# Splitting MoE weight chunks into two halves on ScalarE and VectorE alone, without GpSimd

## The chip, the cores and the metric

The kernel runs on one core of one Trainium2 chip. The metric is the device time of one execution in microseconds. Before the change the median of three runs is 1549.79 us (1549.74 to 1550.39).

## What is computed

The reference chains three layers on 1792 tokens (4 sequences of 448) with a model width of 768:

```python
scores = einsum('bhij,hg->bgij', scale * q @ k.T, w_pre)   # attention, heads mixed
attn   = softmax(scores); attn = einsum('bhij,hg->bgij', attn, w_post); x = attn @ v
expert_idx = argmax(x @ w_gate, axis=1)                    # MoE, top 1 of 8 experts
out[mask]  = gate_w * (maximum(x[mask] @ w1[e], 0) @ w2[e])
g = h * sigmoid(h); y = g @ w_out      # h = out @ w_in     # dense FFN, width 2048
```

All inputs are float32. To keep accuracy on TensorE, every operand of a large product is split in two: a high half rounded to the fp32r type, and a low half, which is the operand minus its high half. A product is then three matmuls (`mm3`, lines 797 to 799: high by high, high by low, low by high).

## The kernel before, in words

The program has three stages: attention (its instruction order comes from a list scheduler, class `Plan`), the MoE layer and the dense FFN (both in `experts`, in the order in which the code is written).

In the MoE stage tokens are sorted by expert and worked on in tiles of 128, called slots; 18 slots are run. A slot needs four weight chunks of its expert: c = 0 and 1 are the two halves of `w1[e]` (products `mm1`, 18 matmuls of 512 columns each), c = 2 and 3 the two halves of `w2[e]` (`mm2`, 24 matmuls of 384 columns). A pair (slot, c) is an item. `slots` writes the items out in a fixed order: for a slot s of the middle it is (s, 0), (s-1, 2), (s, 1), (s-1, 3).

Each chunk has one raw buffer (`wraw`, 128 x 3072 floats) into which SP loads it (`wload`, line 842); where the next slot has the same expert, the load is skipped by a condition. A load is issued as soon as the chunk's predecessor in that buffer has been split. `wsplit` (lines 849 to 856) splits a raw chunk in two steps of 1536 columns (`HW`), each into a pair of tiles, `rhi` and `rlo`, from a ring of four pairs. `ahead` runs the splits two items (LOOK = 4 steps) ahead of the matmuls.

In one step the columns are divided at `PC` = 1152: ACT rounds the first 1152 (line 852) and DVE subtracts them (line 854); POOL rounds the other 384 (line 853) and subtracts them (line 855).

The same engines also do this around the items, in the order of the code:

- PE transposes the gathered tokens (`xT`, 6 transposes, line 872) and the hidden layer (`hT`, 4 each); ACT rounds the result to `xhi` or `hhi` and DVE subtracts to `xlo` or `hlo` (`split`, lines 860 and 861).
- ACT applies relu to a finished `mm1` (h, line 891) and the gate to a finished `mm2` (y, line 909). Each of these waits for the end of its item, and the casts for the item after the next stand behind it in ACT's queue.
- POOL issues the gather of tokens two slots ahead (line 865) and the scatter of a finished y (line 911). There is one buffer for y.
- `hook` places routing tables into the stream: `gate_prep` and `gate_table` near slot 0, `order_prep` (lines 703 to 721 and 786) behind item (1, 3). Later it places the first loads and transposes of the FFN; the loads of y for it are issued from ACT's queue.

Of the kernel before, what the change touches and what calls it, by code (L numbers as in the profile page):

```python
# [9 lines left out]
F32 = mybir.dt.float32  # L10
# [4 lines left out]
ALU = mybir.AluOpType  # L15
# [16 lines left out]

P = dict(GHN=3, TDN=1, CVN=2, RAW=4, DB=2, G=4, GH=3, GL=2, WM=3, E=4, CC=384, GLN=2, WMN=1, slack=0.05, rx=3.2,
         relay=7.0, ghi=3.5, glo=2, mix1=4.6, mx=2.5, exp=3.2, rz=1.9, wm=0.8, ev=3, qk=0.25, qkx=1.85, av=0.5,
         avs=0.7, rows=0.9, tr=-5.8, trh=1.625, trs=0.9, ld=6.1, lv=0.5, c0=-4.0, c1=3.0, cp=0.3, cl=8, PC=1152)


P_WARM = 16
# [42 lines left out]
def fused_kernel(ctx: ExitStack, tc: tile.TileContext, q, k, v, w_pre, w_post, wg, w1, w2, w_in, w_out, cst, out):  # L81
# [30 lines left out]
    with tc.tile_pool(name="pre", bufs=1) as pre:  # L112
# [21 lines left out]
        nc.vector.tensor_tensor(out=wp1l, in0=wp1, in1=wp1h.bitcast(F32), op=ALU.subtract)  # L134
    attention(tc, nc, q, k, v, x_d, oh, cum, zsum, c_e8, ident, (wp1h, wp1l), wp2, wg_sb, ((w_in, wi_d), (w_out, wo_d)))
    experts(tc, nc, x_d, y_d, w1, w2, wi_d, wo_d, out, ident, oh, cum, zsum,
            (tri, c_rid, c_tid, c_val, c_s, c_m), idx_g, idx_s, idx_o, gate_s, es_i)


class Plan:  # L140
    """Orders operations by list scheduling: each engine takes the most urgent operation that can start."""

    LAT = 0.2

# [657 lines left out]
def experts(tc, nc, x_d, y_d, w1, w2, wi_d, wo_d, out, ident, oh, cum, zsum, consts,  # L802
# [7 lines left out]
    with outer:  # L810
# [33 lines left out]
        def pair():  # L844
            return ring.tile([128, HW], F32R, name="rhi", tag="rhi"), ring.tile([128, HW], F32R, name="rlo", tag="rlo")

        PC = P["PC"]

        def wsplit(s, c, half):
            hi, lo = pair()  # L850
            src = raw[c][:, half * HW:(half + 1) * HW]
            nc.scalar.copy(hi[:, :PC], src[:, :PC])  # L852
            nc.gpsimd.tensor_scalar(out=hi[:, PC:], in0=src[:, PC:], scalar1=1.0, scalar2=1.0, op0=ALU.mult, op1=ALU.mult)  # L853
            nc.vector.tensor_tensor(out=lo[:, :PC], in0=src[:, :PC], in1=hi.bitcast(F32)[:, :PC], op=ALU.subtract)  # L854
            nc.gpsimd.tensor_tensor(out=lo[:, PC:], in0=src[:, PC:], in1=hi.bitcast(F32)[:, PC:], op=ALU.subtract)  # L855
            tiles["w", s, c, half] = (hi, lo)

        def split(dst, src):
# [135 lines left out]
        def slots(s0, s1, hook):  # L994
# [7 lines left out]
            def ahead(n):  # L1002
                while nsplit[0] < min(n, 2 * len(plan)):
                    a, c = plan[nsplit[0] // 2]
                    hf = nsplit[0] % 2
                    wsplit(a, c, hf)
                    if hf == 1 and a + 1 < s1:
                        wload(a + 1, c)
                    nsplit[0] += 1
# [123 lines left out]
```

## Time and profile before

| what | value |
|---|---|
| median of three runs | 1549.79 us |
| span of the profiled execution | 1548.0 us |
| attention | from 0 to about 630 us |
| MoE stage, from the first `mm1` to the first FFN matmul | 635 to 1057 us |
| FFN | 1057 to the end |
| mean DMA rate over the span | 121 GB/s |

The page gives the profiled execution by its span; the runs were timed by themselves, and their median is 1.8 us above it. PE is TensorE's matmul, PEld its weight load, which runs beside the matmul before it. A matmul's record is longer than its distance to the next one, because matmuls are pipelined, so gaps are read from the weight loads. Idle time is put down to the event that came last before the engine went on.

### The profile page before, as it was taken

How to read it: one execution, taken by the hardware profiler on the slowest of the kernel's cores; microseconds unless marked ns; L12 is line 12 of the kernel's file. 1: busy time of each engine (PE TensorE's matmuls, PEld its weight loads, DVE VectorE, ACT ScalarE, POOL GpSimd, SP SyncE). 2: the span in 40 equal slices, each digit the busy share in tenths (PEclk: the TensorE clock that was granted, in tenths of full speed). 3: DMA queues.
4: the chain of work that ended last, by engine and by line, in shares of the span. 5: the costliest groups of instructions: out<-in, count | busy, mean ns of one | idle time of the engine just before them, and what ended most of it. 6: DMA issues, size and time to landing. Idle time of an engine off the chain costs nothing. (4 is left out here: it accounts for less than half of the span.)

```text
span 1548.0 us, 25390 instructions
## 1 busy us (share of the span) xinstructions
PE 1441.1 (93%) x9030; PEld 1231.5 (80%) x9030; DVE 1079.0 (70%) x1774; ACT 850.7 (55%) x1600; POOL 811.9 (52%) x877
## 2 busy tenths in 40 slices
PE   7999999999999998897988888988999999999997
PEld 4677667767776777786767667878999999999997
DVE  5798889889998996876766656774445445454464
ACT  4566766677776665354555645653444444444453
POOL 6577577647665774889999998991000000000000
PEclk9999999999999999898999999999999999999999
DMA  7455565656564556205934266407101000010000
GB/s 158 157 159 168 123 213 162 165 147 201 165 149 155 175 164 218 94 21 181 325 104 142 94 229 231 145 11 261 65 11 52 11 31 21 11 42 11 1 31 21
DMA packets 137074, 186.77 MB, mean 121 GB/s; under 512 B 51100, under 2 KB 108736, under 8 KB 136944
## 3 DMA queue, kind: packets, MB, share of 16 engines
q1 hardware_dynamic: 129536, 155.74, 32.8%
q0 software_dynamic: 5392, 23.86, 4.4%
q10 hardware_dynamic: 2016, 5.51, 1.1%
q8 instruction: 73, 1.20, 0.3%
q14 instruction: 57, 0.47, 0.1%
HBM read 186.64 MB, written 30.67 MB: 140 GB/s over the span
## 5 line engine op out<-in xcount | busy, mean ns | idle before, releaser
L854 DVE TENSOR_TENSOR rlo<-wraw,rhi 128x1152 fp32r<-128x1152 f32 x144 | 233.6, 1662 | 127.5 <-ACT rhi L852 127.4
L986 POOL DMA_INDIRECT out_dram<-ob,idx_o x14 | 13.5, 963 | 473.0 <-DVE ob L984 458.5
L855 POOL TENSOR_TENSOR rlo<-wraw,rhi 128x384 fp32r<-128x384 f32 x144 | 204.6, 1421 | 12.0
L423 PE MATMUL m<-WM,E 120*112 120x120 f32 (+1 forms) x1440 | 186.9, 275 | 14.3 <-DVE a_sb L254 6.5
L423 PEld LDWEIGHTS m<-WM,E 120*112 120x112 f32 (+1 forms) x1440 | 162.7, 178 | 41.7 <-issue 18.1
L361 POOL TENSOR_TENSOR GL<-G,GH 120x448 fp32r<-120x448 f32 (+1 forms) x139 | 169.5, 1225 | 11.8 <-ACT GH L254 3.2
L852 ACT CAST rhi<-wraw 128x1152 fp32r<-128x1152 f32 x144 | 158.4, 1151 | 9.6 <-DMA wraw<-in_moe_w_dram 9.6
L797 PE MATMUL b<-fxhi,rhi 128*128 128x384 f32 (+1 forms) x480 | 157.7, 328 | 4.2 <-ACT rhi L860 4.2
L799 PE MATMUL b<-fxhi,rlo 128*128 128x384 f32 (+1 forms) x480 | 157.7, 329 | 0.5 <-DVE rlo L861 0.5
L798 PE MATMUL b<-fxlo,rhi 128*128 128x384 f32 (+1 forms) x480 | 156.8, 327 | 0.0
L956 DVE TENSOR_TENSOR sg<-b,sg 128x384 f32<-128x384 f32 (+1 forms) x80 | 42.4, 530 | 155.6 <-ACT sg L954 155.6
L797 PE MATMUL b<-rhi,gh 128*128 128x384 f32 x436 | 148.4, 340 | 0.0
L954 ACT ACTIVATE sg<-b 128x384 f32<-128x384 f32 (+1 forms) x80 | 37.7, 471 | 199.4 <-PE b L799 199.3
L799 PE MATMUL b<-rhi,gl 128*128 128x384 f32 x436 | 146.8, 337 | 0.0
L798 PE MATMUL b<-rlo,gh 128*128 128x384 f32 x436 | 146.6, 336 | 0.0
L389 ACT ACTIVATE E<-m,mx 120x448 f32<-120x448 f32 x180 | 113.5, 632 | 48.8 <-DVE mx L379 29.6
L410 POOL TENSOR_SCALAR WM<-wp,rz 120x120 f32<-120x120 f32 x180 | 86.3, 487 | 93.0 <-DVE rz L400 40.1
L853 POOL TENSOR_SCALAR rhi<-wraw 128x384 fp32r<-128x384 f32 x144 | 129.1, 897 | 2.6 <-PE b L799 1.7
L798 PE MATMUL b<-rlo,hhi 128*128 128x384 f32 x288 | 101.0, 351 | 20.4 <-POOL rlo L855 20.1
L379 DVE TENSOR_REDUCE mx<-m 120x1 f32<-120x448 f32 x180 | 108.6, 614 | 10.9 <-PE m L799 10.1
L798 PE MATMUL b<-rlo,xhi 128*128 128x512 f32 x216 | 91.1, 422 | 15.8 <-POOL rlo L855 13.4
L797 PE MATMUL b<-rhi,hhi 128*128 128x384 f32 x288 | 100.7, 350 | 1.7 <-POOL rhi L853 1.7
(194 smaller groups left out, 3689.5 us busy)
## 6 DMA issues: line engine op xcount, KB each, us to landing
wraw<-in_moe_w_dram SPq DMA_DIRECT2D x76, 1536.0 KB
G<-S SPq DMA_DIRECT2D x176, 210.0 KB
D<-in_moe_w_in_dram SPq DMA_DIRECT2D x32, 384.0 KB
D<-in_moe_w_out_dram SPq DMA_DIRECT2D x32, 384.0 KB
wi_d<-CM SPq DMA_DIRECT2D x32, 192.0 KB
wo_d<-CM SPq DMA_DIRECT2D x32, 192.0 KB
win<-wi_d SPq DMA_DIRECT2D x8, 768.0 KB
wout<-wo_d SPq DMA_DIRECT2D x8, 768.0 KB
```

The source lines that it names most:

```text
L361: G.tensor_tensor(out=t[:n], in0=x[:n], in1=hi[:n].bitcast(F32), op=ALU.subtract)
L379: V.tensor_reduce(out=mx[:n], in_=tiles["m1", i, g][:n, :S], axis=AX.X, op=ALU.max, negate=True)
L389: A.activation(out=t[:n], in_=tiles.pop(("m1", i, g))[:n, :S], func=ACTF.Exp, bias=tiles.pop(("mx", i, g))[:n], accum_out=tiles["z", i, g ...
L410: G.tensor_scalar(out=wm[:n], in0=wp2[:n], scalar1=rz, scalar2=1.0, op0=ALU.mult, op1=ALU.mult)
L423: nc.tensor.matmul(p[:, c, :, :nr], x[:n, c * CH:(c + 1) * CH], wm[:n, :, :nr], start=True, stop=True)
L797: nc.tensor.matmul(p, lh, rh, start=first, stop=False)
L798: nc.tensor.matmul(p, lh, rl, start=False, stop=False)
L799: nc.tensor.matmul(p, ll, rh, start=False, stop=last)
L852: nc.scalar.copy(hi[:, :PC], src[:, :PC])
L853: nc.gpsimd.tensor_scalar(out=hi[:, PC:], in0=src[:, PC:], scalar1=1.0, scalar2=1.0, op0=ALU.mult, op1=ALU.mult)
L854: nc.vector.tensor_tensor(out=lo[:, :PC], in0=src[:, :PC], in1=hi.bitcast(F32)[:, :PC], op=ALU.subtract)
L855: nc.gpsimd.tensor_tensor(out=lo[:, PC:], in0=src[:, PC:], in1=hi.bitcast(F32)[:, PC:], op=ALU.subtract)
```

## The change

`wsplit` no longer divides the columns. ACT rounds all 1536 columns of a step and DVE subtracts all 1536; POOL's two instructions are gone, and with them the constant `PC`. Everything behind `wsplit` stands four lines earlier in the changed kernel (the subtract is line 851, `split` 856 and 857, the gather 861, the scatter 907).

```diff
-        PC = P["PC"]
-
         def wsplit(s, c, half):
             hi, lo = pair()
             src = raw[c][:, half * HW:(half + 1) * HW]
-            nc.scalar.copy(hi[:, :PC], src[:, :PC])
-            nc.gpsimd.tensor_scalar(out=hi[:, PC:], in0=src[:, PC:], scalar1=1.0, scalar2=1.0, op0=ALU.mult, op1=ALU.mult)
-            nc.vector.tensor_tensor(out=lo[:, :PC], in0=src[:, :PC], in1=hi.bitcast(F32)[:, :PC], op=ALU.subtract)
-            nc.gpsimd.tensor_tensor(out=lo[:, PC:], in0=src[:, PC:], in1=hi.bitcast(F32)[:, PC:], op=ALU.subtract)
+            nc.scalar.copy(hi, src)
+            nc.vector.tensor_tensor(out=lo, in0=src, in1=hi.bitcast(F32), op=ALU.subtract)
             tiles["w", s, c, half] = (hi, lo)
```

POOL, one slot of the MoE stage before the change: a gather, the roundings and subtracts of four chunks, and a scatter in their midst.

```order
L865 DMA xg<-x_d,idx_g 128x768
L853 TENSOR_SCALAR rhi<-wraw_7940 128x384
L855 TENSOR_TENSOR rlo<-wraw_7940,rhi 128x384
L853 TENSOR_SCALAR rhi<-wraw_7940 128x384
...
L855 TENSOR_TENSOR rlo<-wraw_7939,rhi 128x384
L911 DMA y_d<-y,idx_s 1792x768
L853 TENSOR_SCALAR rhi<-wraw_7941 128x384
L855 TENSOR_TENSOR rlo<-wraw_7941,rhi 128x384
```

The same place on POOL in the changed kernel, two slots of it:

```order
L710 TENSOR_SCALAR A_8667<-cs,lo_8662 120x128 x5
L861 DMA xg<-x_d,idx_g 128x768
L907 DMA y_d<-y,idx_s 1792x768
L861 DMA xg<-x_d,idx_g 128x768
L907 DMA y_d<-y,idx_s 1792x768
```

Sixteen instructions of a slot have left POOL's queue; a gather is now directly followed by a scatter.

DVE, the subtracts around item (1, 3) in the changed kernel, up to the first instructions of `order_prep`:

```order
L851 TENSOR_TENSOR rlo<-wraw_7940,rhi 128x1536 x2
L851 TENSOR_TENSOR rlo<-wraw_7942,rhi 128x1536 x2
L857 TENSOR_TENSOR hlo<-b_8545,hhi 128x512
L851 TENSOR_TENSOR rlo<-wraw_7939,rhi 128x1536 x2
L857 TENSOR_TENSOR xlo<-b_8602,xhi 128x384
L857 TENSOR_TENSOR xlo<-b_8608,xhi 128x384
L851 TENSOR_TENSOR rlo<-wraw_7941,rhi 128x1536 x2
L857 TENSOR_TENSOR hlo<-b_8652,hhi 128x512
L703 CAST pi_8659<-pos 120x16
```

Before the change the same rows stand in the same order, with 128x1152 in the subtracts of weights. No instruction of PE, ACT or DVE has changed its place; xlo stands behind both subtracts of a chunk, as before.

## Rows read from the trace of the kernel before

**Rows 1.** The page, busy time by engine over the whole span

```profile
PE 1441.1 (93%) x9030; PEld 1231.5 (80%) x9030; DVE 1079.0 (70%) x1774; ACT 850.7 (55%) x1600; POOL 811.9 (52%) x877
```

**Rows 2.** Windows: length, busy PE, PEld, DVE, ACT, POOL; clock; DMA share; GB/s

```profile
635.00:1057.00 422.00, 364.71 (x1810) 308.01 (x1808) 284.55 (x245) 226.93 (x296) 387.77 (x326) 0.96 0.41 140
858.90:882.50 23.60, 19.90 (x101) 16.27 (x100) 15.70 (x13) 12.54 (x17) 22.56 (x19) 1.00 0.23 79
1066.00:1540.00 474.00, 471.71 (x2819) 470.03 (x2817) 242.82 (x350) 203.79 (x350) 12.52 (x13) 1.00 0.11 38
```

**Rows 3.** Waits of PEld, 635 to 1058 us: total us, times, longest

```profile
PEld b L798 <- POOL rlo L855: 50.8, 46, 2.0
PEld b L797 <- POOL rhi L853: 9.9, 7, 6.3
PEld b L872 <- ACT h L891: 5.4, 2, 3.1
...
PEld b L799 <- DVE xlo L861: 3.3, 9, 0.5
```

**Rows 4.** Timeline, 678 to 694 us: start, length, engine, instruction, idle before it

```profile
678.34 3.20 DVE L854 TENSOR_TENSOR rlo<-wraw,rhi 128x1152 fp32r<-128x1152 f32 x2 [1.13 <-ACT rhi L852]
...
686.70 0.19 PEld L798 LDWEIGHTS b<-rlo,xhi 128*128 128x128 f32 x1 [1.70 <-POOL rlo L855]
...
687.82 0.19 PEld L797 LDWEIGHTS b<-rhi,hhi 128*128 128x128 f32 x1
...
687.97 2.20 ACT L852 CAST rhi<-wraw 128x1152 fp32r<-128x1152 f32 x2
...
689.15 3.43 DVE L854 TENSOR_TENSOR rlo<-wraw,rhi 128x1152 fp32r<-128x1152 f32 x2 [2.76 <-ACT rhi L852]
...
692.42 0.19 PEld L797 LDWEIGHTS b<-rhi,xhi 128*128 128x128 f32 x1
...
693.10 0.19 PEld L799 LDWEIGHTS b<-rhi,xlo 128*128 128x128 f32 x1 [0.37 <-DVE xlo L861]
```

**Rows 5.** Groups of instructions, 635 to 1058 us: busy us, mean ns, idle before

```profile
L854 DVE TENSOR_TENSOR rlo<-wraw,rhi 128x1152 fp32r<-128x1152 f32 x142 | 231.0, 1667 | 126.0 <-ACT rhi L852 125.9
L852 ACT CAST rhi<-wraw 128x1152 fp32r<-128x1152 f32 x142 | 156.2, 1151 | 0.0
...
L861 DVE TENSOR_TENSOR hlo<-b,hhi 128x512 fp32r<-128x512 f32 x36 | 24.4, 677 | 0.0
...
L891 ACT ACTIVATE h<-b 128x512 f32<-128x512 f32 x36 | 21.6, 599 | 101.4 <-PE b L799 85.1 <-DMA y_d<-y,idx_s 16.3
...
L860 ACT CAST hhi<-b 128x512 fp32r<-128x512 f32 x36 | 21.1, 587 | 0.0
...
L861 DVE TENSOR_TENSOR xlo<-b,xhi 128x384 fp32r<-128x384 f32 x36 | 18.2, 543 | 1.1 <-ACT xhi L860 1.1
...
L860 ACT CAST xhi<-b 128x384 fp32r<-128x384 f32 x36 | 15.5, 486 | 2.2 <-PE b L872 2.2
```

**Rows 6.** Groups of instructions in the FFN, 1066 to 1540 us

```profile
L861 DVE TENSOR_TENSOR rlo<-win,rhi 128x768 fp32r<-128x768 f32 x78 | 74.7, 958 | 15.7 <-ACT rhi L860 13.7
...
L860 ACT CAST rhi<-win 128x768 fp32r<-128x768 f32 x78 | 64.9, 833 | 0.0
```

**Rows 7.** Line 854, nanoseconds min/median/max; then line 911, scatter of y

```profile
L854 DVE TENSOR_TENSOR rlo<-wraw,rhi x144: 1343/1652/2179, 631.7 to 1044.8; 128x1152 fp32r<-128x1152 f32 x144
...
DMA to landing us min/median/max: 3.1/4.1/8.1
```

**Rows 8.** Timeline of DVE, `order_prep`: first and last of eight instructions

```profile
697.92 0.40 DVE L703 CAST pi<-pos 120x16 int32<-120x16 f32 x1
...
703.03 0.53 DVE L721 TENSOR_TENSOR B<-sel,tidv 120x224 fp32r<-120x224 f32 x1
```

**Rows 9.** Windows, columns as in rows 2: a stretch in which experts change

```profile
745.00:765.00 20.00, 19.76 (x107) 17.05 (x106) 14.32 (x12) 11.35 (x15) 19.04 (x17) 1.00 0.98 339
```

**Rows 10.** Waits of ACT, 635 to 1058 us

```profile
ACT h L891 <- DMA y_d<-y,idx_s: 16.3, 2, 9.4
```

More of the change, by code (lines that the diff above doesn't have):

```diff
@@ L34 @@
          relay=7.0, ghi=3.5, glo=2, mix1=4.6, mx=2.5, exp=3.2, rz=1.9, wm=0.8, ev=3, qk=0.25, qkx=1.85, av=0.5,
-         avs=0.7, rows=0.9, tr=-5.8, trh=1.625, trs=0.9, ld=6.1, lv=0.5, c0=-4.0, c1=3.0, cp=0.3, cl=8, PC=1152)
+         avs=0.7, rows=0.9, tr=-5.8, trh=1.625, trs=0.9, ld=6.1, lv=0.5, c0=-4.0, c1=3.0, cp=0.3, cl=8)
 P_WARM = 16
```

## The prediction

> **What bounds the kernel now.** I read the page's busy line first: over the whole span TensorE is busy 93%, VectorE (DVE) 70%, ScalarE (ACT) 55%, GpSimd (POOL) 52% [rows 1]. That average hides three stages, so the next view is the table of windows [rows 2]. In the MoE stage, 635 to 1057 us, POOL is busy 388 of 422 us (92%), DVE 285 (67%), ACT 227 (54%). One slot of that stage (an expert tile of 128 tokens, 858.9 to 882.5) takes 23.6 us, and POOL is busy 22.56 us of it. The dense FFN behind it (1066 to 1540) is TensorE without a gap at a granted clock of 1.00; the change does not touch it.
>
> Then the waits of TensorE's weight loads in the MoE stage [rows 3]. All rows of that answer come to 84.7 us; four stand here. 50.8 us, in 46 waits, end with POOL's low-half subtract and 9.9 us with POOL's rounding: 60.7 us for POOL. So without waits the stage would be 422 - 84.7 = 337 us, 18.7 us per slot. One stretch shows that POOL is late alone and not merely last [rows 4]: TensorE starts again at 686.70, after 1.70 us on POOL's subtract. At that time chunk (slot 2, c 1) is being multiplied; DVE took its two low halves from 678.34 to 681.54, five microseconds earlier.
>
> **The change, part by part.** *Removed:* 144 roundings and 144 subtracts of 384 columns on POOL. Only gathers, scatters and five table instructions stay there in this stage, so the waits on POOL go: **-60.7 us**.
>
> *Widened on ACT:* a cast of 1152 columns takes 1151 ns [rows 5], one of 768 takes 833 ns in the FFN [rows 6]: 0.83 ns a column, so 1536 take about 1.47 us, 0.32 more. Per slot 8 x 1.47 + 2 x 0.599 (h) + 2 x 0.587 (hhi) + 2 x 0.486 (xhi) + about 1.2 for the two y (taken as long as h) = 16.3 us, under 18.7.
>
> *Widened on DVE:* the subtract of 1152 takes 1343 ns at least, 1652 in the middle, 2179 at most [rows 7]. In the FFN, where POOL is nearly idle, 768 columns take 958 ns [rows 6]. The line through 958 and 1343 gives 1.74 us for 1536. The upper bound is the stage's mean rate, 1667 ns for 1152 [rows 5], so 2.22 us. I take 1.74, because the low values are those without POOL at work. Per slot: 8 x 1.74 + 2 x 0.677 + 2 x 0.543 [rows 5] = 16.4 us.
>
> Both stay under TensorE's 18.7, but only if the order of the chain holds. I replay one handover [rows 4]. Item (slot 1, c 3) starts at 687.82, my zero. ACT's casts for the item after it, (3, 0), begin at 0.15, and DVE at 1.33, just behind the first cast. With 1536 columns the first cast ends at 1.62, low half A at 3.39, B at 5.14. Item (3, 0) starts at 4.60 (692.42) and wants A at once and B some 2 us later: both are in time. Where fewer transposes lie between two items the margin is smaller by up to 0.8 us, still about 0.4 us. So both engines hide under TensorE; without the cover each slot would cost at most what DVE has over 18.7, which is the first rival.
>
> *What is late next:* xlo. On DVE it stands behind halves A and B. At 693.10 TensorE's third weight load waited 0.37 us for it, and started 5.28 after my zero. Now it comes at 5.14 + 0.54 + 0.06 = 5.74, 0.46 later. Sixteen slots have this place: **+7 us** (0 to +10; zero if TensorE has fallen behind by then anyway).
>
> *The index tables:* eight small DVE instructions from 697.92 to 703.56 [rows 8] stand ahead of slot 2's and 3's subtracts. POOL's table work and splits hid them (one wait on POOL's rounding alone is 6.3 us [rows 3]). They hold DVE 5.6 us; about 1 us of that goes with POOL's splits, and margin and DVE's own idle time cover some 1.5. **+3 us** (0 to +5).
>
> *Weight loads:* a chunk's load is issued when its predecessor is split and has then some 13 us of a slot. An expert's four chunks are 4 x 1536 KB = 6.3 MB, gather and scatter 0.8 MB. In 745 to 765, where experts change in three slots running, DMA moves 339 GB/s at 0.98 busy [rows 9]: 7.1 MB take 20.9 us against a slot of 18.9. Three such slots give 6 us, half of it absorbed by the early issue: **+3 us** (0 to +7).
>
> *Scatter of y:* POOL now issues it at once. It lands 3.1 to 8.1 us after issue [rows 7], and ACT's next write to y comes two items, some 9 us, later, so it just fits. Where ACT itself waits to issue a load of y (16.3 us in two waits [rows 10]), the present loss at TensorE, 5.4 us on h [rows 3], stays. Less POOL traffic beside the gate tables at the start is worth about **-1 us**. The other waits I leave as they are.
>
> Sum: -60.7 + 7 + 3 + 3 - 1 = -48.7. The profiled execution spans 1548.0 us; the median of the runs is 1549.8, so 1.8 us more. 1548.0 - 48.7 + 1.8 = **1501 us**.
>
> One rule speaks against the change. By the rows, POOL has the smallest share of the whole span and the change loads two busier engines. The Trainium skill (Perfetto Trace Analysis, Identifying the Most-Contended Engine) says to relieve the engine with the highest occupancy first; read over the span, it would see nothing to win here, and the time would stay at 1549.8. The same page says that the most contended engine may change between regimes, and [rows 2] show that it does.
>
> **The rivals.** *First, DVE stays slow and becomes the bound.* If the 2179 ns are not POOL's doing but DMA's or the wide tile's, a subtract takes 2.22 us and a slot 8 x 2.22 + 2.44 = 20.2 us, 1.5 more for some 15 slots: 1523 us. For it: the median of 1652 is far over 1343. Against: the 958 ns beside an idle POOL. The Trainium skill (SBUF — State Buffer, Who interferes with whom) says that a DVE instruction with two SBUF inputs and a GpSimd instruction that reads SBUF block each other, the second until the first ends. By that rule the spread is POOL's, and it goes; the trace agrees as far as 1343 to 2179 shows.
>
> *Second, the loads bind at every change of expert.* There are seven such slots; 20.9 against 18.9 plus a late first chunk each, 2 to 3 us: 14 to 18 us more, 1516 us. For: 0.98 busy in [rows 9]. Against: single changes have half the traffic per microsecond.
>
> *Third, slower.* Place: ACT's queue, where the next casts stand behind h or y, which wait for the end of an item. If a split cannot be ready two items ahead, as the four-pair ring intends, each item shows TensorE the chain of cast 1.47 + subtract 1.74 + 0.7 of activation and handover = 3.9 us. Over 72 items that is 281 us in place of 84.7: about 1746 us. It decides where the mean wait of an item passes 84.7 / 72 = 1.18 us. Against it: the replay.
>
> *Fourth, it does not do what it says:* POOL's waits are put down to the last comer, and DVE would be late just behind it: 1549 us. Against: the five microseconds at 681.54.
>
> **How the numbers follow.** Main case 0.72, 1488 (xlo, tables and loads cost nothing) to 1510 (their upper ends): 1501 is its sum. DVE-bound 0.10 at 1523; loads 0.12 at 1516; slower 0.03; nothing 0.03. A change of 0.2% is about what measurement can tell here. The main case and the first two rivals are faster: 0.94; within 0.2%: 0.03; slower: 0.03. The range 1484 to 1524 takes in the first two rivals, and below the main case 4 us of what the half-clock stretches in the stage (0.96 granted on the mean [rows 2]) may give back.
>
> **What would show it.** Right: no waits on POOL in the MoE stage, POOL under 20% busy there; casts at 1.47 and subtracts at 1.74 us; ordinary slots near 19 us; waits on xlo the largest repeated row; a stage of some 373 us; an FFN as long as before. Wrong: subtracts over 2 us, waits on DVE's low half in every slot, ACT waiting for weights, or slots over 20 us where no expert changes.

## The result and the profile after

The changed kernel takes 1488.24 us (median; 1487.63 to 1490.55) against 1550.09 us for the kernel before in the same runs. The ratio is 0.9601, with a 95% interval of 0.9587 to 0.9615: 61.9 us faster. I had forecast 1501 us in a range of 1484 to 1524, so the direction and the range hold, and the gain came out 13 us larger than the sum. One run among all those below, of the kernel with fills, took 2230.30 us at a granted clock of 0.565 and is left out.

The page of the changed kernel, its busy line and two of its rows of 40 slices (compare [rows 1]):

```profile
PE 1421.9 (96%) x9030; PEld 1228.3 (83%) x9030; DVE 1087.4 (73%) x1774; ACT 897.0 (60%) x1600; POOL 487.1 (33%) x589
...
POOL 6576667666665776413211110100000000000000
PEclk9999999999999999999999999999999999999999
```

POOL has lost 325 us, DVE gained 8 and ACT 46. Windows of the changed kernel, columns as in [rows 2]: the MoE stage, an ordinary slot, the FFN.

```profile
638.00:999.00 361.00, 344.30 (x1808) 303.26 (x1808) 291.53 (x247) 271.93 (x295) 64.39 (x39) 0.99 0.48 163
827.90:846.70 18.80, 18.55 (x100) 16.44 (x99) 15.83 (x13) 15.04 (x17) 3.42 (x2) 1.00 0.21 67
...
1008.00:1482.00 474.00, 470.41 (x2812) 468.82 (x2810) 241.76 (x349) 202.62 (x348) 13.59 (x14) 1.00 0.11 39
```

The stage shrinks from 422 to 361 us, an ordinary slot from 23.6 to 18.8; the FFN does the same work in the same time. The whole gain is in the MoE stage. Waits of PEld, 638 to 1001 us (all ten rows of the answer, 27.8 us, against 83.9 before; the 84.7 in the prediction is a slip, its rows come to 83.9):

```profile
PEld b L799 <- DVE xlo L857: 9.2, 14, 0.7
PEld b L798 <- DVE rlo L851: 4.6, 3, 1.6
PEld b L799 <- DVE hlo L857: 3.7, 2, 1.9
PEld b L797 <- ACT rhi L856: 3.0, 1, 3.0
PEld b L931 <- DVE xlo L857: 1.9, 3, 0.6
PEld b L797 <- ACT rhi L850: 1.9, 2, 0.9
PEld b L868 <- ACT h L887: 1.3, 2, 0.8
PEld b L728 <- DVE xlo L857: 1.0, 1, 1.0
PEld b L799 <- DVE rlo L857: 0.7, 1, 0.7
PEld b L797 <- ACT xhi L856: 0.5, 1, 0.5
```

POOL has left the list, which [rows 3] led with 60.7 us. xlo leads, as forecast. The two widened instructions, nanoseconds min/median/max:

```profile
L851 DVE TENSOR_TENSOR rlo<-wraw,rhi x144: 1747/1753/1843, 634.6 to 991.7; 128x1536 fp32r<-128x1536 f32 x144
```
```profile
L850 ACT CAST rhi<-wraw x144: 1455/1472/1491, 633.1 to 989.8; 128x1536 fp32r<-128x1536 f32 x144
```

The subtract handles a third more columns in hardly more time than the mean 1667 ns of [rows 5], and its spread (1343 to 2179 in [rows 7]) is gone. The handover that the prediction replayed, in the changed kernel (timeline; the item before the wait starts at 842.11):

```profile
842.11 0.19 PEld L797 LDWEIGHTS b<-rhi,hhi 128*128 128x128 f32 x1
...
842.25 2.84 ACT L850 CAST rhi<-wraw 128x1536 fp32r<-128x1536 f32 x2
...
843.75 3.43 DVE L851 TENSOR_TENSOR rlo<-wraw,rhi 128x1536 fp32r<-128x1536 f32 x2 [0.59 <-ACT rhi L850]
...
846.71 0.19 PEld L797 LDWEIGHTS b<-rhi,xhi 128*128 128x128 f32 x1
...
847.70 0.19 PEld L799 LDWEIGHTS b<-rhi,xlo 128*128 128x128 f32 x1 [0.69 <-DVE xlo L857]
```

From the item's start: DVE begins at 1.64 us (replay 1.65), low half B is done at 5.07 (5.14), the next item starts at 4.60 (4.60) and its third weight load at 5.59 (5.74).

### The profile page after: what moved, and what is told of

Its sections match the earlier page's. It is cut to its first block, busy times and chain, and to the rows that moved or that the text cites. A ratio compares the mean times of both kernels' runs of the same rounds, so it can differ in the third digit from the quotient of the medians.

```text
span 1488.8 us, 24900 instructions
## 1 busy us (share of the span) xinstructions
PE 1421.9 (96%) x9030; PEld 1228.3 (83%) x9030; DVE 1087.4 (73%) x1774; ACT 897.0 (60%) x1600; POOL 487.1 (33%) x589
## 5 line engine op out<-in xcount | busy, mean ns | idle before, releaser
L851 DVE TENSOR_TENSOR rlo<-wraw,rhi 128x1536 fp32r<-128x1536 f32 x144 | 246.7, 1756 | 65.2 <-ACT rhi L850 65.0
L850 ACT CAST rhi<-wraw 128x1536 fp32r<-128x1536 f32 x144 | 204.7, 1472 | 9.4 <-DMA wraw<-in_moe_w_dram 9.4
L423 PEld LDWEIGHTS m<-WM,E 120*112 120x112 f32 (+1 forms) x1440 | 164.9, 180 | 40.2 <-issue 18.8
L907 POOL DMA_INDIRECT y_d<-y,idx_s x18 | 18.3, 1016 | 282.1 <-ACT y L905 253.6
L799 PE MATMUL b<-rhi,hlo 128*128 128x384 f32 x288 | 97.0, 337 | 3.0 <-DVE hlo L857 3.0
L798 PE MATMUL b<-rlo,hhi 128*128 128x384 f32 x288 | 96.8, 336 | 0.0
L443 PE MATMUL tp<-a_sb,v_sb 128*64 128x120 f32 (+1 forms) x1536 | 95.1, 267 | 0.6 <-ACT a_sb L254 0.6
```

The costliest lines, as they stand in the source:

```text
L423: nc.tensor.matmul(p[:, c, :, :nr], x[:n, c * CH:(c + 1) * CH], wm[:n, :, :nr], start=True, stop=True)
L443: nc.tensor.matmul(p[ro:ro + 64, oo:oo + m], v_sb[:, g, c, :], a_sb[i % 2][:, c, g, :m], start=(c == 0), stop=(c == 3))
L798: nc.tensor.matmul(p, lh, rl, start=False, stop=False)
L799: nc.tensor.matmul(p, ll, rh, start=False, stop=last)
L850: nc.scalar.copy(hi, src)
L851: nc.vector.tensor_tensor(out=lo, in0=src, in1=hi.bitcast(F32), op=ALU.subtract)
```

## The experiments

The theories: **Q** (queue), TensorE waited because the columns it needed stood at the end of a long queue on POOL; **P** (port), POOL and DVE made each other slow while both read; **G**, gathers and scatters behind POOL's splits were what mattered. The last four runs test terms of the sum and look for a better version.

### Work on POOL that nothing reads

Edit in the changed kernel, in a helper that is called after DVE's subtract (`seen` is a constant tile, `aside` is never read):

```diff
+            nc.gpsimd.tensor_scalar(out=aside, in0=seen, scalar1=1.0, scalar2=1.0, op0=ALU.mult, op1=ALU.mult)
+            nc.gpsimd.tensor_tensor(out=aside, in0=seen, in1=seen, op=ALU.subtract)
```

> The changed kernel, with a rounding and a subtract of 384 columns put back on POOL in every split step, on a constant tile, with a result that nothing reads. Theory Q (queue: before, TensorE waited for results that stood at the end of POOL's long queue): nobody waits for these, so within 8 us of the changed kernel's 1488, POOL as busy as before. Theory P (port: POOL was slow, and DVE with it, because each blocks the other while both read): DVE's subtracts go from 1.75 to about 2.2 us, a slot from 18.8 to some 20.2, the whole to 1505 to 1525. Theory G (the gain came from gathers and scatters that no longer stand behind POOL's splits): above 1520 and like the kernel with writes only.

The second kernel fills `aside` (four times `nc.gpsimd.memset(aside, 0.0)`) in place of the two.

> The changed kernel, with four zero fills of 384 columns on POOL in every split step (no reads, about as long as the two instructions with an idle DVE, 1.6 us), in a tile that nothing reads. Q: 1488 to 1496. P: DVE's subtracts stay at 1.75 us, so 1488 to 1496, clearly under the kernel with reads. G: as far above 1488 as the kernel with reads.

With reads: 1584.59 us, ratio 1.0218 [1.0181, 1.0255], slower than the kernel before. With fills: 1500.68 us (median of three), 0.9658 [0.9619, 0.9696], some 5 us over what Q and P expected. Groups of instructions, 638 to 1000 us, of the kernel with reads:

```profile
L859 DVE TENSOR_TENSOR rlo<-wraw,rhi 128x1536 fp32r<-128x1536 f32 x114 | 226.7, 2030 | 96.2 <-ACT rhi L858 96.0
L853 POOL TENSOR_TENSOR aside<-seen 128x384 fp32r<-128x384 f32 x114 | 160.9, 1412 | 9.5
...
L852 POOL TENSOR_SCALAR aside<-seen 128x384 fp32r<-128x384 f32 x115 | 122.1, 1062 | 8.3
```

and of the kernel with fills:

```profile
L857 DVE TENSOR_TENSOR rlo<-wraw,rhi 128x1536 fp32r<-128x1536 f32 x141 | 241.5, 1755 | 73.0 <-ACT rhi L856 70.0 <-issue 3.1
L851 POOL MEMSET aside<- 128x384 f32 x564 | 238.0, 422 | 30.6
```

Reading is what hurts. On the mean DVE's subtract goes from 1756 to 2030 ns beside reads and stays at 1755 beside fills, and POOL's own two take 2.47 us a step (531 and 830 ns at the median of all, so both are fast when not blocked), where the four fills take 1.69. P is right on the mechanism and much too small in price; Q, which expected no effect from unread work, falls for the kernel with reads, and G, which expected both kernels alike, falls too. What the fills cost stands at one place: ACT waits 11.9 us for a scatter of y (at 730.79) and TensorE 8.0 us for the weight cast behind it. How so much time can be lost where nobody reads POOL's result is shown by ACT's waits, 638 to 1085 us, in the kernel with reads:

```profile
ACT y L914 <- DMA y_d<-y,idx_s: 58.3, 7, 13.2
...
ACT h L896 <- DMA y_d<-y,idx_s: 18.6, 3, 9.8
```

and by the largest wait of PEld, 636 to 1100 us:

```profile
PEld b L797 <- ACT rhi L858: 39.5, 10, 9.3
```

From 700 to 900 us POOL is busy 188 of 200 us there:

```profile
700.00:900.00 200.00, 160.48 (x780) 141.38 (x780) 143.31 (x103) 116.52 (x124) 187.84 (x146) 0.90 0.48 160
```

The scatter of y stands in its queue; with one buffer, ACT can't write the next y, and the weight casts stand behind it in ACT's queue. Waits are not all of it. From the first `mm1` to the first FFN matmul this kernel takes 453.0 us, 92 more than the changed kernel (361.0); its weight loads wait 69 us more (95.9 against 26.6), and the other 23 us are work that ran slower, at a granted clock of 0.90 on the mean against 0.99:

```profile
640.28:1093.24 452.96, 371.71 (x1808) 325.20 (x1808) 335.29 (x246) 270.96 (x295) 417.61 (x326) 0.90 0.39 129
```

I tried whether the buffer alone is to blame:

```diff
-                tiles["y", s] = xp.tile([128, DM], F32, name="y", tag="y", bufs=1)
+                tiles["y", s] = xp.tile([128, DM], F32, name="y", tag="y", bufs=2)
```

> The kernel with unread rounding and subtract on POOL (1584.6 us), with two buffers for y in place of one. There ACT waited 58.3 us for scatters before its writes of y. If that kernel's loss hangs on y's one buffer, POOL being late but able to keep up: 1500 to 1530. If POOL's throughput is the pace (22 us busy in an ordinary slot of 23.4, so gathers and scatters fall further behind whatever buffers there are): 1555 to 1590, with the waits moved to gathers or to the second next y.

One look: 1573.69 us beside 1552.3 of the kernel before. The waits move, they don't go: POOL's throughput is the pace. Waits of PEld, 638 to 1085 us, where now the transposes (L877) of gathered tokens and of h lead (each of the five put down to issue ends 0.1 us behind the landing of a gather):

```profile
PEld b L877 <- issue: 25.6, 5, 6.0
PEld b L877 <- ACT h L896: 20.0, 3, 14.8
```

So POOL is a bound by its queue, and the queue is long because of blocking: in the kernel before, a slot's eight steps at 2.32 us (897 + 1421 ns on its page) are 18.5 of POOL's 22.6 us, and at 1.55 us unblocked they would be 12.4, an estimate. Q and P are one chain, and late gathers and scatters are a second way by which it reaches TensorE.

### POOL keeps a part of the work

Half of its columns, in the kernel before:

```diff
-         ... cl=8, PC=1152)
+         ... cl=8, PC=1344)
```

> The kernel before with PC = 1344: POOL keeps 192 of 1536 columns and TensorE still waits for them. Q: POOL's work per step halves (0.53 + 1.02 to some 0.9 us without blocking), POOL is no bound any more: 1488 to 1500. P: each of POOL's instructions still waits for a subtract of DVE (1.55 us long, up to 2.2 when blocked itself), so POOL stays near 18 to 20 us a slot: 1505 to 1535.

1503.56 us, 0.9685 [0.9657, 0.9714]: between the two forecasts. POOL's instructions, 638 to 1000 us on the mean, then min/median/max of all:

```profile
L855 POOL TENSOR_TENSOR rlo<-wraw,rhi 128x192 fp32r<-128x192 f32 x140 | 134.0, 957 | 11.7
L853 POOL TENSOR_SCALAR rhi<-wraw 128x192 fp32r<-128x192 f32 x140 | 106.7, 762 | 23.2 <-PE b L799 22.3
```
```profile
L853 POOL TENSOR_SCALAR rhi<-wraw x144: 341/360/1702, 634.1 to 1003.7; 128x192 fp32r<-128x192 f32 x144
L855 POOL TENSOR_TENSOR rlo<-wraw,rhi x144: 588/603/1972, 635.0 to 1004.1; 128x192 fp32r<-128x192 f32 x144
```

Half the columns take 1.72 us a step instead of 2.32: a quarter less, not half. From 830 to 849 us POOL is busy 18.0 of 19.0 us and TensorE 18.9: POOL just fits under it.

```profile
830.00:849.00 19.00, 18.91 (x101) 16.57 (x100) 15.50 (x13) 13.77 (x16) 18.00 (x18) 1.00 0.36 113
```

Only the rounding left on POOL (DVE subtracts all 1536), and then only the subtract (ACT rounds all 1536):

```diff
-            nc.vector.tensor_tensor(out=lo[:, :PC], in0=src[:, :PC], in1=hi.bitcast(F32)[:, :PC], op=ALU.subtract)
-            nc.gpsimd.tensor_tensor(out=lo[:, PC:], in0=src[:, PC:], in1=hi.bitcast(F32)[:, PC:], op=ALU.subtract)
+            nc.vector.tensor_tensor(out=lo, in0=src, in1=hi.bitcast(F32), op=ALU.subtract)
```

> The kernel before with POOL only rounding its 384 columns; DVE subtracts all 1536. ACT casts 1152. Q: POOL's queue is 8 x 0.53 + 3 = some 7 us a slot: 1485 to 1495. P: each rounding can stand behind a subtract of 1.75 us and the subtract of DVE waits for the rounding, so the chain gets longer by up to 1.75 us: 1495 to 1530, with waits on POOL's rounding in DVE's and TensorE's rows.

```diff
-            nc.scalar.copy(hi[:, :PC], src[:, :PC])
-            nc.gpsimd.tensor_scalar(out=hi[:, PC:], in0=src[:, PC:], scalar1=1.0, scalar2=1.0, op0=ALU.mult, op1=ALU.mult)
+            nc.scalar.copy(hi, src)
```

> The kernel before with ACT rounding all 1536 columns; POOL keeps the subtract of 384, DVE subtracts 1152. If one blocked POOL instruction a step is short enough: POOL at 8 x 1.4 + 3 = some 14 us a slot, 1490 to 1505, like the kernel in which POOL only rounds. If TensorE still waits for the end of POOL's subtract in most items: 1515 to 1545.

1499.99 us, 0.9656 [0.9627, 0.9685], as P had it, and 1503.64 us in one look, inside its first forecast. Either half of POOL's work can stay and most of the gain is there. In both, POOL's instruction about doubles: the rounding takes 1087 ns on the mean, the subtract 2001, where the medians before were 528 and 1020. In all three kernels with a part left on POOL, most of what is lost against the changed kernel is lost at one place, between 709 and 714 us, where POOL's splits stand behind its five instructions for the index tables: a wait of 6.2 us on POOL's rounding with 192 columns, of 7.3 us on DVE's low half with the rounding, of 6.1 us on POOL's subtract. Their stages are 11 to 13 us longer, 7 to 8 of them there; waits are 4.5 to 7.7 us of it, and the rest is again work at a lower granted clock (0.96 to 0.97 in the stage).

### Two terms of the sum, and a better version

All weight loads made, none skipped:

```diff
-            nc.sync.dma_start(out=chunk_dst(c), in_=chunk_src(c, regs[s, 0]), cond=regs[s, 1], cond_hint=False)
+            nc.sync.dma_start(out=chunk_dst(c), in_=chunk_src(c, regs[s, 0]))
```

> The changed kernel with every weight load made (no condition), 72 chunks in place of some 28, so 7.1 MB in every slot. The prediction's term for the loads rests on 339 GB/s as the limit: 20.9 us a slot against 18.8, some 17 slots more than 2 us each: 1520 to 1530. If the DMA can go faster than that stretch showed (the early issue lets two loads overlap all the time), 18.8 us hold and it stays under 1500. If a load comes to be waited for by its full length, over 1560.

One look: 1511.35 us, between the first two forecasts, and not for the reason that the first gave. Windows of this kernel, columns as in [rows 2], the middle of the stage:

```profile
800.00:820.00 20.00, 19.75 (x109) 17.63 (x108) 17.32 (x14) 16.23 (x18) 3.42 (x2) 1.00 1.03 368
820.00:840.00 20.00, 19.75 (x107) 17.64 (x106) 16.44 (x14) 16.24 (x18) 3.42 (x2) 1.00 1.04 380
```

TensorE keeps its 18.8 us a slot with DMA full all the time, at 368 to 380 GB/s. Most of what is lost stands at the start: ACT waits 24.7 us for weights, in three waits, all before 660 us, against 9.4 in the changed kernel, and at the 91st weight load of the stage TensorE is 16 us behind the changed kernel, of 22 at the start of the FFN. At the start of the stage the four chunks loaded ahead of it are loaded once more.

xT ahead of the weight splits, in the changed kernel:

```diff
                 (mm1 if c < 2 else mm2)(a, c)
+                if s0 < a < last and c == 1:
+                    xT(a + 1)
                 ahead(2 * n + 2 + LOOK)
...
-                if s0 < a < last and c == 1:
-                    xT(a + 1)
```

> The changed kernel with the transposes and the split of the next slot's tokens (xT) placed ahead of the weight splits of the same item. Theory O (xlo is late only because it stands behind both subtracts on DVE): the 9.2 us of waits on xlo go, no others come, since the casts' start moves by 0.97 us and low half A then lies 0.3 us ahead of its need: 1477 to 1482. Rival M (the margin is eaten): waits on the low half or on ACT's rounding take their place, 1486 to 1492.

The FFN's loads of y from POOL's queue:

```diff
-            nc.scalar.dma_start(out=x, in_=y_d[t0:t0 + 128, :])
+            nc.gpsimd.dma_start(out=x, in_=y_d[t0:t0 + 128, :])
```

> The changed kernel with the FFN's loads of y issued from POOL's queue in place of ACT's, so that ACT no longer waits for the scatter of y that stands ahead of the load. In the changed kernel two such waits hold ACT for 10.4 us and show at TensorE as 1.3 us on h, and behind it on rounding and low halves, some 6 us in all. Theory A (these follow from ACT's wait): 1481 to 1484. Rival: the next write of y or the loads are late anyway: 1487 to 1490.

> Both edits together. O and A right and their places apart: the sum of both gains, 1470 to 1477. If they share waits: as the better of the two alone, 1478 to 1484.

xT first: 1484.20 us, ratio to the kernel before 0.9567 [0.9515, 0.9619], between O and M; the waits on xlo fall from 9.2 to 0.9 us, but h rises from 1.3 to 3.0, and the interval overlaps that of the changed kernel, so its worth alone is not settled. Loads from POOL: 1482.49 us, 0.9547 [0.9506, 0.9587]; the weight rounding and h leave the list and the low half falls from 4.6 to 1.3 us, as theory A had it; the interval ends where that of the changed kernel begins. Both: 1471.40 us, 0.9485 [0.9446, 0.9524], clear of the changed kernel: 16.8 us less, more than the 4.0 and 5.7 of the two alone, and inside the 1470 to 1477 forecast for separate places. The traces show where the two help each other: with xT first alone, TensorE gains some 7 us by 868 us and loses 4 there, at a wait of 2.2 us on h and in the stretch behind it (granted clock 0.61 from 868.7 to 876.0); with the loads on POOL that wait is gone, and the 7 us stay. Waits of PEld in the stage of this best kernel, the largest three of five:

```profile
PEld b L797 <- ACT rhi L856: 2.6, 1, 2.6
PEld b L799 <- DVE hlo L857: 2.1, 2, 1.8
PEld b L798 <- DVE rlo L851: 1.9, 1, 1.9
```

and an ordinary slot of it, 18.3 us of TensorE without a gap:

```profile
820.00:838.30 18.30, 18.30 (x100) 16.54 (x99) 15.84 (x12) 15.05 (x17) 3.43 (x3) 1.00 0.14 43
```

## Why the prediction was right, and where its sum was off

- **The bound and the waits removed** were read rightly: the 60.7 us on POOL went, and no run with POOL's work shortened was slower than before. That POOL alone was late, seen in [rows 4], held. With 83.9 us of waits in place of 84.7 the stage without them is 338 us, 18.8 a slot, which is what an ordinary slot now takes.
- **ACT and DVE.** 1.47 and 1.74 us were forecast (the line through 958 and 1343 gives 1.73), 1.472 and 1.753 measured. The choice of the low end for DVE is shown by the fills: beside writes it stays at 1.755, beside reads it rises to 2.03. The first rival (2.22 us) is out.
- **Weight loads**, +3 us: this term failed. It took the 339 GB/s of one stretch [rows 9] for a limit. The kernel before already moves more at the start of its FFN (windows, columns as in [rows 2]):

```profile
1060.00:1080.00 20.00, 20.00 (x109) 19.97 (x108) 9.47 (x14) 7.97 (x13) 0.00 (x0) 0.91 1.05 372
```

  The run that makes every load moves up to 380 GB/s over the middle of the stage and holds 18.8 us a slot; no wait for a weight load shows in the changed kernel behind the first.

The other terms are read against rows of the kernel before that [rows 3] leave out:

```profile
PEld b L797 <- ACT rhi L860: 4.5, 1, 4.5
PEld b L798 <- DVE rlo L854: 3.4, 3, 1.4
...
PEld b L728 <- issue: 2.8, 1, 2.8
PEld b L797 <- ACT rhi L852: 1.2, 2, 0.6
PEld b L799 <- DVE hlo L861: 0.9, 1, 0.9
PEld b L728 <- DVE xlo L861: 0.7, 1, 0.7
...
PEld b L935 <- DVE xlo L861: 0.3, 1, 0.3
```

- **xlo** was forecast at +7 us and came at +5.9 (3.3 to 9.2). Ahead of the FFN's first transposes and of a table lookup, for which the sum had no term, it cost 1.9 more (1.0 to 2.9).
- **Index tables**, +3 us: mis-sized. One wait of 1.35 us on DVE's low half stands at that place (701.98), where 0.9 stood before: +0.5.
- **Loads of y**: I said that the 5.4 us on h stay. But TensorE also waits for the weight rounding and the low half behind h at the same two places: 9.2 us in all before (near 919 and 965 us), 6.4 after, of which h is 1.3. So 2.8 us went, and reading the row on h alone missed the rest. Loads from POOL take all of it away.
- **Gate tables**, -1 us: no row gave this term its size, and nothing came of it. The wait of 2.8 us there is gone, and waits on hlo beside it rise as much (0.9 to 3.7).
- **Not in the sum:** the granted clock. In the stage it rises from 0.96 to 0.99: some 30 us of it stood at the lower of the two levels (1.2 GHz) before, some 7 after. At that level the weight loads of `mm1` follow each other by 0.43 us (713 to 717 us, kernel before), at 2.4 GHz by 0.23. The stage shrank by 60.6 us (421.6 to 361.0 between the first `mm1` and the first FFN matmul) and the waits in that stretch by 56.9 (83.5 to 26.6), so 3.7 us lie in work that ran faster. The clock is the likely cause, since the kernels with more of the stage at the lower level also have the slower work; no run held it fixed. I had this only as 4 us at the low end of the range.

The stage beats the sum by 11.9 us: 3 (loads) + 2.5 (index tables) + 2.8 (loads of y) + 1.1 (xlo) + 3.7 (work) + 1.5 (the wait on ACT at the start of the FFN, 4.5 to 3.0) is 14.6; 1.9 (xlo elsewhere) and 1 (gate tables) go against it, and 0.2 is left. The measured time lies at the lower end of the main case (1488 to 1510): the added costs were too high, and the range held because its low end let most of them be nothing.

The rule on the most-contended engine (the Trainium skill, Perfetto Trace Analysis, Identifying the Most-Contended Engine), read over the whole span, would have kept POOL in the work; read by stage it points at POOL, and the measurement agrees. The rule on the shared port (the Trainium skill, SBUF — State Buffer, Who interferes with whom) says that a DVE instruction with two SBUF inputs contends with GpSimd's reads and not with its writes: the two kernels with unread work show just that, 2030 against 1755 ns.

## What to carry to other kernels

Read the shares of the engines by stage: an engine at half of the whole span can be the bound of the stage that matters. A third engine that takes a quarter of the columns is no help if it and the second block each other: count its instructions at their blocked duration, here 2.3 us and not 1.55, and add what else stands in its queue. Compare two kernels by the length of a stage and its granted clock too, not by waits alone: in the kernel with reads 23 of the 92 us were no waits. When the wait goes, look for the next in-order queue: here the best version came from moving two things out of the way of ACT and DVE, not from faster instructions.

## What was not expected of the hardware

Blocking is paid per instruction, not per column. Unblocked, a step's two instructions on POOL take 1.55 us with 384 columns and 0.96 with 192 (medians: 528 + 1020 and 360 + 603 ns); on the mean they take 2.32 and 1.72, so blocking adds 0.77 and 0.76.

And the gather of tokens on POOL became slower when POOL became idle: line 861 takes 944 to 2632 ns, median 2400, where the same gather before had a median of 1042, while the scatter takes 982 to 1043. What decides is whether it starts while DVE runs a weight subtract. Of the 72 gathers and scatters of the two kernels, 31 do; they take 1.97 to 2.63 us, and each ends 0.84 to 0.95 us behind the end of that subtract. The other 41 take 0.94 to 1.12 us. Before, 6 gathers and 11 scatters were caught; in the changed kernel 14 of 18 gathers start some 0.2 us after DVE has begun, and no scatter does. One gather caught in each kernel (the subtract around the first stands in [rows 4]), and a scatter that was not:

```profile
679.21 1.98 POOL L865 DMA_INDIRECT xg<-x_d,idx_g  x1 [0.15 <-issue]
```
```profile
866.25 1.02 POOL L907 DMA_INDIRECT y_d<-y,idx_s  x1 [15.09 <-ACT y L905]
...
867.37 3.43 DVE L851 TENSOR_TENSOR rlo<-wraw,rhi 128x1536 fp32r<-128x1536 f32 x2 [0.44 <-ACT rhi L850]
867.57 2.40 POOL L861 DMA_INDIRECT xg<-x_d,idx_g  x1 [0.30 <-issue]
```

So the subtract holds it up; this was read from two traces and not tried by itself. It costs the changed kernel nothing, since the gather runs two slots ahead.
